# Attention with keys, queries and results stored half by half, and the last inverse moved beside the value products of the first half

## The chip, the cores and the metric

The kernel runs on one core of one Trainium2 chip. The metric is the device time in microseconds (us) of one execution. Before the change, three runs took 573.23, 575.68 and 578.89 us, a median of 575.68 us. A difference of about 1% is what a measurement of this kernel can tell from no change.

## The reference

Two independent problems share one launch, and their outputs are concatenated: A in columns 0 to 639, B in columns 640 to 1279.

```python
def _A_ref(x, wqkv, wo):                 # x 1x2048x640, wqkv 640x1920, wo 640x640
    H = 32; Dh = D // H                  # 32 heads of 20
    W, dil = 8, 2                        # 8 keys: positions s, s-2, ..., s-14
    q, k, v = split of (x @ wqkv)
    idx = pos[:, None] - off[None, :]
    mask = idx >= 0
    logits = einsum("bhsd,bhswd->bhsw", q, kg) * scale
    logits = where(mask, logits, -1e9)
    attn = softmax(logits, axis=-1)
    o = einsum("bhsw,bhswd->bhsd", attn, vg)
    return o @ wo

def _B_ref(u, A_re, A_im, B_re, B_im, C_re, C_im, log_dt, Dskip):
    P = exp(dt * A * l)                  # a 2048-tap filter per channel, from 192 modes
    K = einsum("dn,dnl,dn->dl", C, P, dt * B).real
    y = irfft(rfft(u padded) * rfft(K padded))[:L]
    return y + u * Dskip
```

## The kernel before

**The two problems in time.** Problem B comes first: for five chunks of channels the filter is made from tables (about the first 360 us of the profiled execution), its transform and that of `u` are multiplied, and the first part of the inverse (`ia`, line 419) leaves a tensor `Z` that is written to memory as `Zdram`. The second part of the inverse (`ib`, line 566) reads it back in blocks called `zq` and adds the result into `u`. Problem A (class `Attention`, line 599) begins beside the last chunk of B: `x` is loaded and transposed into `xa` (tag `X0`) and `xb` (tag `S8`), and the keys and queries of the first half are projected beside the last `ia`.

**Halves.** The 2048 positions are four segments of 512 that sit side by side in partition groups of 32 heads. Each segment is cut into half 0 (its first 256 positions) and half 1. A key window reaches back 14 positions (`HALO`). `proj_k` (656) and `proj_q` (677) project one half in ten steps each, every step being five matmuls of 128x512 and one copy out of PSUM. For half 0, `proj_k` has five more short steps for the last 14 keys of every segment. `kT` and `qT` hold both halves of a segment in one run of 512 positions.

**`Attention.run` (787) sets the order.** (1) `logits(0, w)` (698) for the eight window positions w: VectorE multiplies queries by shifted keys into `prod` (128x5120, two places, tags `X1` and `M`), and TensorE sums over head elements into `ps_l`. These are interleaved with `other`, which is the 22 steps of `ib`, and then with the ten key steps of half 1. (2) The ten query steps of half 1. (3) `softmax(0)` (713) and `logits(1, w)`, interleaved with the 20 value projections `proj_v(d)` (688). All values go into one tile `v2` (tag `u`), and one DMA then fills its halo. (4) `av(0, b, w)` (751), with `softmax(1)` between the first steps: VectorE multiplies values by weights into `prod2` (three places, tags `Ssp`, `WK`, `A1`), and TensorE sums over w into `ps_o`. There are three blocks b of 8, 8 and 4 head elements, with eight w each. (5) `av(1)`, interleaved with the eight `out_proj` steps (774) of half 0. (6) The `out_proj` steps of half 1, which end the kernel.

**What sets the order on the engines.** `interleave` (342) mixes two lists of steps evenly. The tile framework then fixes one order of instructions for each engine, which can differ a little from the written one, and puts waits where a tile is read, written or its place reused. PSUM is one pool of eight banks in this part (tag `bank`): the logits of a half hold four, the value sums of a block hold four, and `ps_ib`, `ps_qk`, `ps_v` and `ps_op` take what is left.

**`ib` before.** Each step (three positions of 64, 22 steps) is 3 matmuls with the identity, 24 short ones with `H`, and a copy to `u`, by ScalarE and VectorE in turn (`Evac(nc, "ad")`, 562). Every fourth step loads a `zq` block by five DMAs of 192 KB on SyncE's queue. Six blocks share two places (tags `Ssp`, `WK`), so block n + 2 waits until block n is used up. After steps l = 30 and l = 63, four DMAs write `u` to the output.

```python
interleave([self.logits(0, w) for w in range(W)], other + rest)   # 794
for st in self.proj_q(1, new, ev): st()                           # 795
...
interleave(l1, [self.proj_v(d) for d in range(DH)])               # 809
...
for i, st in enumerate(av(0)):                                    # 816
    st()
    if i % 2 == 1 and i < 8: sm[1 + i // 2]()
interleave(av(1), op(0))                                          # 821
```

Of the kernel before, what the change touches and what calls it, by code (L numbers as in the profile page):

```python
# [18 lines left out]
NCH = 5  # L19
# [414 lines left out]
def partB(tc, pools, prm, B_u, B_Dskip, out_b, att):  # L434
# [164 lines left out]
class Attention:  # L599
# [42 lines left out]
    def load_w(self):  # L642
        nc, ar = self.nc, self.ar
        self.w = {}
        for i, nm, tag in ((1, "k", "WU"), (0, "q", "MX"), (2, "v", "R")):
            t = self.w[nm] = ar.tile([128, 5, D], bf16, name="w" + nm, tag=tag)
            nc.sync.dma_start(out=t[:], in_=self.wsrc[:, :, D * i:D * i + D])
        self.kT = ar.tile([128, 5, HALO + S], bf16, name="kT", tag="Y1")
        nc.gpsimd.memset(self.kT[:, :, 0:HALO], 0.0)
        self.qT = ar.tile([128, 5, S], bf16, name="qT", tag="Y0")  # L650

    def proj(self, w, ct, rhs, ps):
        for kt in range(5):
# [2 lines left out]
    def proj_k(self, hf, new, ev):  # L656

        x4 = lambda kt: self.xs(kt).rearrange("p (s i) -> p s i", s=4)

        def part(ct, sp):  # L660
            def run():
                ps = new()[:].rearrange("p (s i) -> p s i", s=2)
                self.proj("k", ct, lambda kt: x4(kt)[:, 2 * sp:2 * sp + 2, 256 * hf:256 * hf + 256], ps)
                n = 256 - HALO * hf
                k4 = self.kT[:, ct, HALO:HALO + S].rearrange("p (s i) -> p s i", s=4)
                ev(k4[:, 2 * sp:2 * sp + 2, 256 * hf:256 * hf + n], ps[:, :, 0:n])
            return run

        def halo(ct):
            def run():  # L670
                ps = new()[:, 0:4 * HALO].rearrange("p (s i) -> p s i", s=4)
                self.proj("k", ct, lambda kt: x4(kt)[:, :, 512 - HALO:512], ps)
                ev(self.kT[:, ct, HALO:HALO + S].rearrange("p (s i) -> p s i", s=4)[:, :, 512 - HALO:512], ps)
            return run
        return [part(ct, sp) for ct in range(5) for sp in range(2)] + ([halo(ct) for ct in range(5)] if hf == 0 else [])

    def proj_q(self, hf, new, ev):
        x4 = lambda kt: self.xs(kt).rearrange("p (s i) -> p s i", s=4)

        def part(ct, sp):  # L680
            def run():
                ps = new()[:].rearrange("p (s i) -> p s i", s=2)
                self.proj("q", ct, lambda kt: x4(kt)[:, 2 * sp:2 * sp + 2, 256 * hf:256 * hf + 256], ps)
                ev(self.qT[:, ct].rearrange("p (s i) -> p s i", s=4)[:, 2 * sp:2 * sp + 2, 256 * hf:256 * hf + 256], ps)
            return run
        return [part(ct, sp) for ct in range(5) for sp in range(2)]

    def proj_v(self, d):
        def run():
            ps = self.bank("ps_v")  # L690
            for kt in range(5):
                for sc in range(4):
                    self.nc.tensor.matmul(ps[32 * sc:32 * sc + 32, :], lhsT=self.w["v"][:, kt, d:D:DH], rhs=self.xs(kt)[:, 512 * sc:512 * sc + 512],  # L693
                                          start=(kt == 0), stop=(kt == 4), tile_position=(0, 32 * sc), skip_group_check=True)
            self.nc.scalar.copy(out=self.v2[:, d, HALO:HALO + 512], in_=ps[:])
        return run

    def logits(self, hf, w):
        def run():
            if w == 0:  # L700
                self.lps[hf] = [self.bank("ps_l", [128, 2, 256]) for _ in range(4)]
            q4 = self.qT[:].rearrange("p c (s i) -> p c s i", s=4)
            k4 = self.kT[:, :, HALO - DIL * w:HALO - DIL * w + S].rearrange("p c (s i) -> p c s i", s=4)
            pr = self.ar.tile([128, 5, 4, 256], bf16, name="prod", tag=("X1", "M")[w % 2])
            hs = slice(256 * hf, 256 * hf + 256)
            self.nc.vector.tensor_tensor(out=pr[:], in0=q4[:, :, :, hs], in1=k4[:, :, :, hs], op=A.mult)  # L706
# [44 lines left out]
    def av(self, hf, b, w):  # L751
# [5 lines left out]
        def run():  # L757
            if w == 0:
                self.ops[(hf, b)] = [self.bank("ps_o", [128, nd // 4, 256]) for _ in range(4)]
            ops = self.ops[(hf, b)]  # L760
            p2 = self.ar.tile([128, 8, 256], bf16, name="prod2", tag=("Ssp", "WK", "A1")[w % 3])
            off = HALO + 256 * hf - DIL * w
            nc.vector.tensor_tensor(out=p2[:, 0:nd], in0=self.v2[:, 8 * b:8 * b + nd, off:off + 256], in1=self.attn[:, hf, w, :].unsqueeze(1).to_broadcast([128, nd, 256]), op=A.mult)  # L763
            for dq in range(4):
                for sc in range(4):
                    sl = slice(32 * sc, 32 * sc + 32)
# [1 line left out]
                                     tile_position=(32 * sc, 32 * dq), skip_group_check=True)  # L768
            if w == W - 1:
                for sc in range(4):  # L770
                    nc.scalar.copy(out=self.o4[:, sc, 2 * b:2 * b + nd // 4, 256 * hf:256 * hf + 256], in_=ops[sc][:])
        return run

    def out_proj(self, hf, sc, q):
        def run():
            s0 = 256 * hf + 128 * q
            ob = self.ar.tile([128, D], bf16, name="ob", tag="PF", bufs=2)
            for eh in range(2):
                ps = self.bank("ps_op", [128, 320])
                for dd in range(5):  # L780
                    self.nc.tensor.matmul(ps[:], lhsT=self.o4[:, sc, dd, s0:s0 + 128], rhs=self.wo[:, dd, 320 * eh:320 * eh + 320], start=(dd == 0), stop=(dd == 4))  # L781
                self.nc.scalar.copy(out=ob[:, 320 * eh:320 * eh + 320], in_=ps[:])
            r0 = 512 * sc + s0
            self.nc.sync.dma_start(out=self.out_a[r0:r0 + 128, :], in_=ob[:])
        return run

    def run(self, psa, other):
# [5 lines left out]
        rest = self.proj_k(1, new, ev)  # L793
# [16 lines left out]
        nc.gpsimd.memset(self.v2[0:32, :, 0:HALO], 0.0)  # L810
        nc.sync.dma_start(out=self.v2[32:128, :, 0:HALO], in_=self.v2[0:96, :, 512:512 + HALO])
# [75 lines left out]
```

## Time and profile before

| | before |
|---|---|
| three runs, us | 573.23, 575.68, 578.89 |
| profiled execution, us | 571.97 |
| its span in the profile, us | 570.2 |
| TensorE matmul busy | 430.1 us, 75% |
| TensorE weight load busy | 266.7 us, 47% |
| VectorE busy | 410.3 us, 72% |
| ScalarE busy | 342.3 us, 60% |
| mean granted TensorE clock | 0.924 |

The profiled execution took 1.8 us more than its span, and it lies 3.7 us under the median of the three runs. Times in views are in us from the start of the span, and a line such as L706 is a line of the kernel before. Of a busy figure, a matmul's end is modelled, so a busy TensorE need not be at its peak. "Idle before" is the time an engine stood still ahead of an instruction, with the instruction that released it.

### The profile page before, as it was taken

To read this page: it belongs to the slowest core of one execution; us is meant where nothing else is said; L and a number is where in the kernel's file an instruction comes from. 1 tells how busy PE (TensorE), PEld (TensorE's weight loads), DVE (VectorE), ACT (ScalarE), POOL (GpSimd) and SP (SyncE) were. 2 spreads that over 40 slices of the span, in tenths; PEclk is the share of its full clock that TensorE was granted. 3 is DMA by queue.
4 is the path that set the end of the run, shared out by engine and by line. 5 is a ranking of instruction groups with operands and counts; after the bars stand their busy time and mean duration, and the time that the engine had idled before them with its cause. 6 is when DMAs were issued, how large, how long until landed. Compare 5 with 4: busy or idle time off the path is not lost.

```text
span 570.2 us, 15418 instructions
## 1 busy us (share of the span) xinstructions
PE 430.1 (75%) x6929; PEld 266.7 (47%) x6929; DVE 410.3 (72%) x501; ACT 342.3 (60%) x449; POOL 35.2 (6%) x49
## 2 busy tenths in 40 slices
PE   0135794798889798888988887899785679835796
PEld 0013463364556465546554555656552347701354
DVE  3574799869886998699976977232962669699880
ACT  2483683979597969595977595375221534421354
POOL 8700000000000000100000000000000000000000
PEclk9999997899899999899997999799798899955799
DMA  4594324350035203612052059205472150000112
GB/s 118 128 162 168 119 76 151 91 137 12 11 82 159 85 6 81 171 56 82 2 175 49 3 183 264 77 6 190 154 177 92 29 108 15 5 2 1 36 56 98
DMA packets 51674, 51.56 MB, mean 90 GB/s; under 512 B 37384, under 2 KB 48328, under 8 KB 48664
## 3 DMA queue, kind: packets, MB, share of 16 engines
q1 hardware_dynamic: 49720, 49.69, 31.9%
q0 software_dynamic: 1184, 0.89, 0.7%
q8 instruction: 54, 0.88, 0.6%
q10 hardware_dynamic: 704, 0.00, 0.1%
q14 instruction: 12, 0.10, 0.1%
HBM read 32.30 MB, written 18.19 MB: 89 GB/s over the span
## 4 chain that ended last, share of the span: by engine, by line
PE 29%; DVE 9%; ACT 7%; issue 6%; DMA 2%; SPq 0%; ACTq 0%; POOL 0%; DVEq 0%
PE ps_qk L654 7%; PE ps_v L693 4%; DVE prod L763 3%; PE ps_k L289 3%; PE ps_op L781 2%; DVE prod L706 2%; PE ps_k L286 2%; PE ps_ib L583 2%; ACT Y L248 2%; PE ps_l L709 2%; ACT X L248 1%; PE ps_ia L426 1%; PE ps_t L202 1%; PE ps_xt L634 1%; PE ps_ib L577 1%
## 5 line engine op out<-in xcount | busy, mean ns | idle before, releaser
L706 DVE TENSOR_TENSOR prod<-qT,kT 128x5120 bf16<-128x5120 bf16 x16 | 44.7, 2822 | 25.1 <-ACT kT L337 14.3
L248 ACT ACTIVATE X<-ps_t 128x1024 bf16<-128x1024 int16 x60 | 60.6, 1045 | 3.0 <-PE ps_t L202 2.3
L248 ACT ACTIVATE Y<-ps_t 128x1024 bf16<-128x1024 int16 x60 | 59.2, 1041 | 1.2 <-PE ps_t L202 0.6
L202 PE MATMUL ps_t<-R,PF 128*128 128x512 f16 (+1 forms) x160 | 51.8, 421 | 8.4 <-ACT X L248 3.7
L286 PE MATMUL ps_k<-Y,X 128*32 128x64 bf16 x1280 | 51.8, 294 | 2.1 <-issue 1.8
L289 PE MATMUL ps_k<-Y,X 64*32 64x64 bf16 x1280 | 47.7, 291 | 4.4 <-issue 2.4
L763 DVE TENSOR_TENSOR prod<-v,attn 128x2048 bf16<-128x2048 bf16 (+1 forms) x48 | 46.8, 1039 | 3.2 <-PE ps_o L767 2.7
L202 PE MATMUL ps_t<-R,PM 128*128 128x256 f16 (+4 forms) x120 | 23.4, 299 | 33.0 <-DMA PM<-scr 22.5
L337 DVE CAST A<-ps_f 128x1024 bf16<-128x1024 f32 x28 | 34.2, 1220 | 15.4 <-PE ps_f L376 15.2
L337 ACT CAST Ssp<-ps_f 128x1024 bf16<-128x1024 f32 x26 | 26.5, 1021 | 30.5 <-PE ps_f L387 23.1
L289 PEld LDWEIGHTS <-X 64*32 64x32 bf16 x1280 | 34.5, 109 | 19.3 <-issue 16.8
L286 PEld LDWEIGHTS <-X 128*32 128x32 bf16 x1280 | 34.2, 109 | 18.1 <-issue 11.6
L254 DVE TENSOR_TENSOR Y<-Y,M 128x2048 bf16<-128x2048 bf16 x30 | 36.6, 1219 | 6.1 <-ACT Y L248 6.0
L767 PE MATMUL ps_o<-prod,ident 32*32 32x512 bf16 (+1 forms) x768 | 22.5, 453 | 23.8 <-DVE prod L763 23.7
L376 PE MATMUL ps_f<-BD,u 128*64 128x128 bf16 x320 | 23.1, 296 | 22.9 <-DVE A L337 10.3
L256 DVE TENSOR_TENSOR Y<-Y,M 128x2048 bf16<-128x2048 bf16 x30 | 36.6, 1221 | 0.4
L260 DVE TENSOR_TENSOR X<-X,MX 128x2048 bf16<-128x2048 bf16 x30 | 36.6, 1219 | 0.2
L222 ACT ACTIVATE M<-ps_t 128x1024 bf16<-128x1024 f32 x30 | 30.0, 1026 | 8.8 <-DVE Y L256 4.3
L376 PEld LDWEIGHTS <-u 128*64 128x64 bf16 x320 | 20.8, 204 | 27.3 <-issue 27.1
L205 PE MATMUL ps_t<-R,PF 128*64 128x512 f16 (+1 forms) x160 | 25.4, 384 | 5.5 <-ACT Y L248 3.4
L202 PEld LDWEIGHTS <-PM 128*128 128x128 f16 (+1 forms) x120 | 8.6, 102 | 42.8 <-DMA PM<-scr 22.5
L337 DVE CAST Ssp<-ps_f 128x1024 bf16<-128x1024 f32 x14 | 17.1, 1220 | 12.6 <-PE ps_f L387 12.6
(150 smaller groups left out, 852.6 us busy)
## 6 DMA issues: line engine op xcount, KB each, us to landing
Udram<-Ssp SPq DMA_DIRECT2D x5, 1024.0 KB
U<-Udram SPq DMA_DIRECT2D x5, 1024.0 KB
Uw<-Udram SPq DMA_DIRECT2D x10, 512.0 KB
Zdram<-Z SPq DMA_DIRECT2D x5, 1024.0 KB
zq<-Zdram SPq DMA_DIRECT2D x25, 192.0 KB
u<-in_B_u_dram SPq DMA_DIRECT2D x4, 640.0 KB
xn<-in_A_x_dram SPq DMA_DIRECT2D x4, 640.0 KB
out_dram<-ob SPq DMA_DIRECT2D x16, 160.0 KB
```

Source lines behind the costliest of these rows:

```text
L202: MM(ps, lhsT=Pt[0:K, 2 * blk + th, 0:128], rhs=rhs[0:K], start=True, stop=True, skip_group_check=True)
L248: order(nc.scalar.activation(out=dst, in_=ps[:].bitcast(i16)[:, :, 0::2], func=ACT.Sin, scale=SINSC))
L254: V.tensor_tensor(out=hi, in0=lo, in1=m(0), op=A.mult)
L256: V.tensor_tensor(out=lo, in0=lo, in1=m(2), op=A.mult)
L260: V.tensor_tensor(out=xf, in0=xf, in1=mx, op=A.mult)
L286: MM(o, lhsT=X[:, r, g, t], rhs=Y[:, r, g, :, t], start=(k == 0 and r == 0), stop=False, tile_position=(0, 32 * g), skip_group_check=True)
L289: MM(o, lhsT=X[hb:hb + 64, r, 4 + g % 2, t], rhs=Y[hb:hb + 64, r, 4 + g % 2, :, t], start=False, stop=(r == 1), tile_position=(hb, 32 * g) ...
L337: ins = self.nc.scalar.copy(out=out, in_=in_) if e == "a" else self.nc.vector.tensor_copy(out=out, in_=in_)
L376: MM(ps[64 * r:64 * r + 64, i], lhsT=src_fn(8 * q + i), rhs=BD[:, r], start=(i % 4 == 0), stop=True, skip_group_check=True, tile_position= ...
L654: self.nc.tensor.matmul(ps, lhsT=self.w[w][:, kt, 128 * ct:128 * ct + 128], rhs=rhs(kt), start=(kt == 0), stop=(kt == 4))
L706: self.nc.vector.tensor_tensor(out=pr[:], in0=q4[:, :, :, hs], in1=k4[:, :, :, hs], op=A.mult)
L763: nc.vector.tensor_tensor(out=p2[:, 0:nd], in0=self.v2[:, 8 * b:8 * b + nd, off:off + 256], in1=self.attn[:, hf, w, :].unsqueeze(1).to_bro ...
```

## The change

- `kT`, `qT` and `o4` get an outer index for the half, so each half is a separate run of memory. The keys of half 1 get their own 14 halo columns, which one new ScalarE copy (`mid`, 128x280) fills from half 0; the short key steps cover three segments instead of four.
- `ib` leaves the first stage: `logits(0)` is now interleaved with the ten key and the ten query steps of half 1, and `ib` is interleaved with `av(0)` and `softmax(1)`.
- `zq` now uses the places of `xa` and `xb` (`X0`, `S8`). Every copy of `ib` to `u` is now ScalarE's.
- `v2` becomes three tiles (8, 8 and 4 head elements, tags `Ssp`, `WK`, `MX`), each with its own halo DMA as soon as it is full. `prod2` uses `X1`, `M` and `Y1`.

```diff
-    evy = Evac(nc, "ad")
+    evy = Evac(nc, "a")
-                zt[0] = z = ar.tile([...], name="zq", tag=("Ssp", "WK")[l // NP % 2])
+                zt[0] = z = ar.tile([...], name="zq", tag=("X0", "S8")[l // NP % 2])
-        self.kT = ar.tile([128, 5, HALO + S], bf16, name="kT", tag="Y1")
+        self.kT = ar.tile([128, 2, 5, 4, HALO + 256], bf16, name="kT", tag="Y1")
-        self.qT = ar.tile([128, 5, S], bf16, name="qT", tag="Y0")
+        self.qT = ar.tile([128, 2, 5, 4, 256], bf16, name="qT", tag="Y0")
+        def mid():
+            self.nc.scalar.copy(out=self.kT[:, 1, :, :, 0:HALO], in_=self.kT[:, 0, :, :, 256:256 + HALO])
-            self.nc.scalar.copy(out=self.v2[:, d, HALO:HALO + 512], in_=ps[:])
+            if d % 8 == 0:
+                self.v2.append(self.ar.tile([128, min(8, DH - d), HALO + 512], bf16, name="v2", tag=("Ssp", "WK", "MX")[d // 8]))
+            v2 = self.v2[d // 8]
+            self.nc.scalar.copy(out=v2[:, d % 8, HALO:HALO + 512], in_=ps[:])
+            if d in (7, 15, 19):
+                self.nc.gpsimd.memset(v2[0:32, :, 0:HALO], 0.0)
+                self.nc.sync.dma_start(out=v2[32:128, :, 0:HALO], in_=v2[0:96, :, 512:512 + HALO])
-            p2 = self.ar.tile([128, 8, 256], bf16, name="prod2", tag=("Ssp", "WK", "A1")[w % 3])
+            p2 = self.ar.tile([128, 8, 256], bf16, name="prod2", tag=("X1", "M", "Y1")[w % 3])
-        interleave([self.logits(0, w) for w in range(W)], other + rest)
-        for st in self.proj_q(1, new, ev):
-            st()
+        interleave([self.logits(0, w) for w in range(W)], self.proj_k(1, new, ev) + self.proj_q(1, new, ev))
+        a0 = []
         for i, st in enumerate(av(0)):
-            st()
+            a0.append(st)
             if i % 2 == 1 and i < 8:
-                sm[1 + i // 2]()
+                a0.append(sm[1 + i // 2])
+        interleave(a0, other)
-        self.o4 = ar.tile([128, 4, 5, 512], bf16, name="o4", tag="Y0")
+        self.o4 = ar.tile([128, 2, 4, 5, 256], bf16, name="o4", tag="Y0")
```

More of the change, by code (lines that the diff above doesn't have):

```diff
@@ L569, in run @@
                 np_ = min(NP, 64 - l)
-                zt[0] = z = ar.tile([128, NCH, 2 * NP, 32], bf16, name="zq", tag=("Ssp", "WK")[l // NP % 2])
+                zt[0] = z = ar.tile([128, NCH, 2 * NP, 32], bf16, name="zq", tag=("X0", "S8")[l // NP % 2])
                 for c in range(NCH):
@@ L647, in load_w @@
             nc.sync.dma_start(out=t[:], in_=self.wsrc[:, :, D * i:D * i + D])
-        self.kT = ar.tile([128, 5, HALO + S], bf16, name="kT", tag="Y1")
-        nc.gpsimd.memset(self.kT[:, :, 0:HALO], 0.0)
-        self.qT = ar.tile([128, 5, S], bf16, name="qT", tag="Y0")
+        self.kT = ar.tile([128, 2, 5, 4, HALO + 256], bf16, name="kT", tag="Y1")
+        nc.gpsimd.memset(self.kT[:, 0, :, 0, 0:HALO], 0.0)
+        self.qT = ar.tile([128, 2, 5, 4, 256], bf16, name="qT", tag="Y0")
     def proj(self, w, ct, rhs, ps):
@@ L663, in run @@
                 self.proj("k", ct, lambda kt: x4(kt)[:, 2 * sp:2 * sp + 2, 256 * hf:256 * hf + 256], ps)
-                n = 256 - HALO * hf
-                k4 = self.kT[:, ct, HALO:HALO + S].rearrange("p (s i) -> p s i", s=4)
-                ev(k4[:, 2 * sp:2 * sp + 2, 256 * hf:256 * hf + n], ps[:, :, 0:n])
+                ev(self.kT[:, hf, ct, 2 * sp:2 * sp + 2, HALO:HALO + 256], ps)
             return run
@@ L670, in run @@
             def run():
-                ps = new()[:, 0:4 * HALO].rearrange("p (s i) -> p s i", s=4)
-                self.proj("k", ct, lambda kt: x4(kt)[:, :, 512 - HALO:512], ps)
-                ev(self.kT[:, ct, HALO:HALO + S].rearrange("p (s i) -> p s i", s=4)[:, :, 512 - HALO:512], ps)
-            return run
-        return [part(ct, sp) for ct in range(5) for sp in range(2)] + ([halo(ct) for ct in range(5)] if hf == 0 else [])
+                ps = new()[:, 0:3 * HALO].rearrange("p (s i) -> p s i", s=3)
+                self.proj("k", ct, lambda kt: x4(kt)[:, 0:3, 512 - HALO:512], ps)
+                ev(self.kT[:, 0, ct, 1:4, 0:HALO], ps)
+            return run
+        def mid():
+            self.nc.scalar.copy(out=self.kT[:, 1, :, :, 0:HALO], in_=self.kT[:, 0, :, :, 256:256 + HALO])
+        return [part(ct, sp) for ct in range(5) for sp in range(2)] + ([halo(ct) for ct in range(5)] if hf == 0 else [mid])
     def proj_q(self, hf, new, ev):
@@ L683, in run @@
                 self.proj("q", ct, lambda kt: x4(kt)[:, 2 * sp:2 * sp + 2, 256 * hf:256 * hf + 256], ps)
-                ev(self.qT[:, ct].rearrange("p (s i) -> p s i", s=4)[:, 2 * sp:2 * sp + 2, 256 * hf:256 * hf + 256], ps)
+                ev(self.qT[:, hf, ct, 2 * sp:2 * sp + 2], ps)
             return run
@@ L701, in run @@
                 self.lps[hf] = [self.bank("ps_l", [128, 2, 256]) for _ in range(4)]
-            q4 = self.qT[:].rearrange("p c (s i) -> p c s i", s=4)
-            k4 = self.kT[:, :, HALO - DIL * w:HALO - DIL * w + S].rearrange("p c (s i) -> p c s i", s=4)
             pr = self.ar.tile([128, 5, 4, 256], bf16, name="prod", tag=("X1", "M")[w % 2])
-            hs = slice(256 * hf, 256 * hf + 256)
-            self.nc.vector.tensor_tensor(out=pr[:], in0=q4[:, :, :, hs], in1=k4[:, :, :, hs], op=A.mult)
+            self.nc.vector.tensor_tensor(out=pr[:], in0=self.qT[:, hf], in1=self.kT[:, hf, :, :, HALO - DIL * w:HALO - DIL * w + 256], op=A.mult)
             for ct in range(5):
@@ L760, in run @@
             ops = self.ops[(hf, b)]
-            p2 = self.ar.tile([128, 8, 256], bf16, name="prod2", tag=("Ssp", "WK", "A1")[w % 3])
+            p2 = self.ar.tile([128, 8, 256], bf16, name="prod2", tag=("X1", "M", "Y1")[w % 3])
             off = HALO + 256 * hf - DIL * w
-            nc.vector.tensor_tensor(out=p2[:, 0:nd], in0=self.v2[:, 8 * b:8 * b + nd, off:off + 256], in1=self.attn[:, hf, w, :].unsqueeze(1).to_broadcast([128, nd, 256]), op=A.mult)
+            nc.vector.tensor_tensor(out=p2[:, 0:nd], in0=self.v2[b][:, :, off:off + 256], in1=self.attn[:, hf, w, :].unsqueeze(1).to_broadcast([128, nd, 256]), op=A.mult)
             for dq in range(4):
@@ L770, in run @@
                 for sc in range(4):
-                    nc.scalar.copy(out=self.o4[:, sc, 2 * b:2 * b + nd // 4, 256 * hf:256 * hf + 256], in_=ops[sc][:])
+                    nc.scalar.copy(out=self.o4[:, hf, sc, 2 * b:2 * b + nd // 4], in_=ops[sc][:])
         return run
@@ L775, in run @@
         def run():
-            s0 = 256 * hf + 128 * q
+            s0 = 128 * q
             ob = self.ar.tile([128, D], bf16, name="ob", tag="PF", bufs=2)
@@ L780, in run @@
                 for dd in range(5):
-                    self.nc.tensor.matmul(ps[:], lhsT=self.o4[:, sc, dd, s0:s0 + 128], rhs=self.wo[:, dd, 320 * eh:320 * eh + 320], start=(dd == 0), stop=(dd == 4))
+                    self.nc.tensor.matmul(ps[:], lhsT=self.o4[:, hf, sc, dd, s0:s0 + 128], rhs=self.wo[:, dd, 320 * eh:320 * eh + 320], start=(dd == 0), stop=(dd == 4))
                 self.nc.scalar.copy(out=ob[:, 320 * eh:320 * eh + 320], in_=ps[:])
-            r0 = 512 * sc + s0
+            r0 = 512 * sc + 256 * hf + s0
             self.nc.sync.dma_start(out=self.out_a[r0:r0 + 128, :], in_=ob[:])
@@ L792, in run @@
         ev = Evac(nc, "a")
-        rest = self.proj_k(1, new, ev)
-        interleave([self.logits(0, w) for w in range(W)], other + rest)
-        for st in self.proj_q(1, new, ev):
-            st()
+        interleave([self.logits(0, w) for w in range(W)], self.proj_k(1, new, ev) + self.proj_q(1, new, ev))
         self.wo = ar.tile([128, 5, D], bf16, name="wo4", tag="WU")
@@ L800, in run @@
             nc.sync.dma_start(out=self.wo[32 * dq:32 * dq + 32], in_=wsrc[dq])
-        self.v2 = ar.tile([128, DH, HALO + 512], bf16, name="v2", tag="u")
+        self.v2 = []
         sm = self.softmax(0)
@@ L809, in run @@
         interleave(l1, [self.proj_v(d) for d in range(DH)])
-        nc.gpsimd.memset(self.v2[0:32, :, 0:HALO], 0.0)
-        nc.sync.dma_start(out=self.v2[32:128, :, 0:HALO], in_=self.v2[0:96, :, 512:512 + HALO])
-        self.o4 = ar.tile([128, 4, 5, 512], bf16, name="o4", tag="Y0")
+        self.o4 = ar.tile([128, 2, 4, 5, 256], bf16, name="o4", tag="Y0")
         av = lambda hf: [self.av(hf, b, w) for b in range(3) for w in range(W)]
```

## The prediction

> **What bounds the kernel now.** I read the groups of instructions by line first, then the chain of work that ended last, then VectorE's timeline from 400 us on, then busy time and granted clock in stretches. Everything before 400 us (tables, transforms, first half's projections) keeps its instructions but for a few short ones, so the sum is about the last 170.2 us (399.96 to 570.2).
>
> From the groups (count, busy us, mean ns, then idle before and its releasers):
>
> ```profile
> L706 DVE TENSOR_TENSOR prod<-qT,kT 128x5120 bf16<-128x5120 bf16 x16 | 44.7, 2822 | 25.1 <-ACT kT L337 14.3
> L763 DVE TENSOR_TENSOR prod<-v,attn 128x2048 bf16<-128x2048 bf16 (+1 forms) x48 | 46.8, 1039 | 3.2 <-PE ps_o L767 2.7
> ```
>
> VectorE lost 25.1 us ahead of the key products, 14.3 us of it to ScalarE's copies into `kT`. The chain shows where:
>
> ```profile
> 425.57 2.17 PE ps_qk L654 x10
> 427.77 0.57 ACT kT L337
> 428.36 2.83 DVE prod L706
> ...
> 433.60 0.57 ACT kT L337
> 434.21 2.13 PE ps_qk L654 x5
> 436.37 0.57 ACT kT L337
> 436.98 1.25 PE ps_qk L654 x5
> 438.26 0.57 ACT kT L337
> 438.87 1.25 PE ps_qk L654 x5
> 440.14 0.57 ACT kT L337
> 440.74 2.84 DVE prod L706
> ```
>
> Two things are seen. Products of half 0 (428.36, 440.74) wait for key copies of half 1, since both lie in one run of `kT`. And TensorE and ScalarE alternate (1.25 + 0.57, a step each 1.88 us instead of 1.08): only one PSUM bank is left, because six banks hold `ib` steps whose `zq` is not there yet (they run at 457.21, 128 matmuls in 2.32 us). VectorE's timeline around it:
>
> ```profile
> 428.36 2.82 DVE L706 TENSOR_TENSOR prod<-qT,kT 128x5120 bf16<-128x5120 bf16 x1 [4.72 <-ACT kT L337]
> 440.74 2.83 DVE L706 TENSOR_TENSOR prod<-qT,kT 128x5120 bf16<-128x5120 bf16 x1 [9.55 <-ACT kT L337]
> ...
> 465.91 8.30 DVE L706 TENSOR_TENSOR prod<-qT,kT 128x5120 bf16<-128x5120 bf16 x3 [4.72 <-ACT qT L337]
> ...
> 515.05 17.48 DVE L763 TENSOR_TENSOR prod<-v,attn 128x2048 bf16<-128x2048 bf16 x19
> ```
>
> So the stretch from 399.96 to 465.91 (66.0 us) is bound by nothing but waits: VectorE is busy 39.8 us in it. From 465.9 to 495.4 TensorE is nearly full (25.9 of 29.4 us); from 495.4 to 554 VectorE is (55.7 of 58.6 us), with TensorE at 34.8 us.
>
> **The change part by part.** The orders of instructions that the two kernels give each engine show that the eight products of half 0 now wait on no ScalarE copy of `kT`.
>
> *Stage A, logits of half 0 with 20 projections.* TensorE again starts at 402.84, after the first product (399.96 + 2.84). It then does 20 steps of 1.08 us (five matmuls; 425.57: ten in 2.17) and eight sums of 0.66 us: 21.6 + 5.3 = 26.9. Its clock is half after the 3.6 us idle, as the row below shows until 408, which adds 2.4. That is 432.1, plus 0.6 for the last query copy. VectorE's eight products (22.6 us) hide beside it. Softmax 0's first three rows (2.34) stand ahead of the first product of half 1, after the last sum, so that starts at 433.2 instead of 465.91: -32.7. Bounds: with a full clock 1.8 less; at 1.88 us a step, as at 438.26 to 440.14, 16 more. I take the nearer end: no `ib` holds a bank here, so four remain.
>
> *Stage B, logits of half 1, softmax 0, value projections.* Softmax 0 was hidden in stage A's idle time; here VectorE has no such cover. It has 8 x 2.83 = 22.6, and of softmax (2 x 2.34 trees, 2.29, 1.75, 2.29 = 11.0) all but the first 2.34: 31.3, say 31.5, to 464.7. TensorE (20 x 1.08 + 8 x 0.55 = 26.0, plus about 5 of waiting for products and half clock) ends at 466.4. Before it was 29.5 (465.91 to 495.44): +2.0. The values no longer wait for the output DMAs of `u` before their copies (the first sum is done near 470.6, its copy starts at 479.25), but TensorE worked on; worth nothing. Bounds of the stage: +1.8 (31.3 alone) to +4.5 (TensorE's half clock lasting as long again as the 2.4 of stage A). The halo DMA (3.13 us at 496.50) lay beside VectorE's tree and subtraction (495.44 to 500.18) and is worth nothing either; its three successors come earlier, the last one behind two `zq` issues on SyncE's queue, some 20 us before it is needed.
>
> *Stage C, value products of half 0, softmax 1, `ib`.* `ib` costs TensorE 22 x 0.84 us (0.31 + 0.53) = 18.5 us, and ScalarE 22 x 0.56 = 12.3. VectorE loses its 11 copies (6.6 us), which had stood in stage A. VectorE has, to the end of block 1 of half 1, 32 x 1.13 + 8 x 0.6 + 11.0 = 52.0 and remains the bound, if `zq` comes in time. `zq` was loaded ahead at 386.67; now it cannot be issued before the last value projection is done with `xa`. The row to price it: five issues from 409.27, use at 415.82, so 6.5 us from release to use. Block 0 is released at 466.2, there at 472.7 to 473.7. ScalarE meets a new wait: the first `ib` copy stands ahead of softmax 1's exponential, which VectorE's later products wait for. But VectorE has three products, half a tree, two products and the subtraction (10.3) until 475.0, and the first copy is over at 475.2, so this costs 0.2. Behind that, blocks 2 and 3 land at 483.7 and 490, ahead of their use. Block 4 is late: SyncE first issues the four output DMAs of `u` (4.54 us at 418.73), so it is issued at 494.4 and lands at 500.9, block 5 at 501.5. TensorE's order has 128 `ib` matmuls (2.32 us, more at half clock) between the halves of the first products of half 1, so VectorE, three places ahead, stands from 502.8 to 506.4: 3.6 us. Sum: 52.0 + 3.6 + 1.9 of older gaps (the 1.91 at 534.44 falls in the same place, others remain) = 57.5 against 54.5 (495.44 to 549.95): +3.0. Bounds: -3.6 when `zq` is in time; above, see the rivals.
>
> *Stage D, block 2 of half 1.* Before, 6.05 us pass from 549.95 to the last copy of `ps_o` (556.0), with two or three output steps beside it. In the new order ScalarE copies blocks 0 and 1 back to back, and six of the eight output steps of half 0 come after block 1. The tail does eight such steps in 11.6 us: 2.05 + 6 x 1.33 + 1.2 = 11.2, +5.0 (between 0 and +6). The tail from there (14.2 us) is the same.
>
> *Small.* `mid` (128x280 on ScalarE, nearest row the 128x256 copies at 0.3) may push the last transform by 0.4. Fewer halo columns and contiguous rows: nothing, since a product of 5120 takes 2.82 us from strided rows already.
>
> Sum: -32.7 + 2.0 + 3.0 + 5.0 + 0.4 = -22.3. On the profiled execution (571.97) that is 549.7; its median of runs lies 3.7 higher, so I say 553.
>
> **A rule against the row.** After idling, and at light load, TensorE runs at half clock here (columns: stretch, length, busy and count of TensorE, weight loads, VectorE, ScalarE, GpSimd, clock, DMA, GB/s):
>
> ```profile
> 404.00:406.00 2.00, 2.00 (x43) 1.72 (x43) 2.00 (x2) 0.00 (x0) 0.00 (x0) 0.50 0.20 75
> 416.00:418.00 2.00, 2.00 (x78) 1.36 (x68) 1.43 (x2) 0.56 (x1) 0.00 (x0) 1.00 0.82 290
> 516.00:520.00 4.00, 2.25 (x64) 0.60 (x64) 4.00 (x5) 0.00 (x0) 0.00 (x0) 0.50 0.00 0
> ```
>
> The Trainium skill, TensorE: Matmul & The Clock Gate, section "Part 1: The HAM clock gate (the "warmup" mystery)", says that the throttled state is the default and that only a window of about 3.4 us of sustained activity lifts it. Read strictly it speaks against stage C, whose bursts never fill a window: `ib` would stay at half clock. By the rule the sum would be -22.3 + 4.1 = -18 (4.1 is worked out under rival 1 from rows), by the row at 416 the -22 above. The rest does not need this paragraph.
>
> **The rivals.**
> 1. *Half clock throughout stage C.* For it: 0.50 at 516 to 520 with 2.25 of 4 us busy. Against: 1.00 at 416 with `ib` in the stream. Price: an `ib` step at half clock is 1.35 (48 matmuls in 1.78 at 405.08, identities 0.45), so 22 x 1.35 + 16 x 0.66 + 8 x 0.44 = 43.8 from 466.4, and VectorE resumes at 510.5 instead of 506.4: about 557.
> 2. *`zq` bound.* Each place is refilled twice behind its use; at 10 us instead of 6.5, three loads on one place cost 10.5: about 563. Against: nothing else loads then.
> 3. *Banks again.* Projections at 1.88 us in stage A: 553 + 16 = 569. Against: nothing holds banks.
> 4. *Better.* No `zq` stall and no bunched output steps: -3.6 and -5.0, about 544.5.
> 5. *Slower than before.* The `zq` refill again, one mechanism: the place `X0` is loaded three times in series, so the gain of 22.3 is gone at 6.5 + 22.3 / 3 = 13.9 us a load, and beyond that it is slower; at 16 us it is 582. Against: twice the only turn-around that the trace shows.
>
> That the change does not do what it says is rival 3: the wait on `kT` is gone by the order, the pace need not be.
>
> **How the numbers follow.** Likeliest 0.57 (own range 547 to 559), rival 1 0.12, rival 2 0.10, rival 3 0.05, rival 4 0.13, rival 5 0.03. The range leaves out rivals 3 and 5 and the far ends of 2 and 4: 544 to 564. All but rival 5 and a part of 3 are faster by over 1% (about what a measurement of this kernel can tell from no change): faster 0.95, same 0.02, slower 0.03.
>
> **What would show it.** Right: no idle before L706 by `kT`; the first product of half 1 near 433, the first value product near 465, block 1 of half 1 done near 522; one stop of 3 to 4 us in VectorE near 503, released by `ib`. Wrong: steps of 1.9 us in stage A (rival 3); clock 0.5 from 475 to 500 (rival 1); TensorE waiting for `zq` several times (rivals 2, 5); VectorE stopping at the tree of softmax 1, if the first `zq` lands after 475.

## The result, and the profile after

The kernel after took 551.39 us (median of four runs, 547.59 to 553.15) beside 574.45 us of the kernel before (four runs): a ratio of 0.9619, 95% interval 0.9526 to 0.9712. Two more series gave 0.9666 (0.9594 to 0.9738) and 0.9649 (0.9615 to 0.9683), so by these ratios the gain is 19 to 22 us. One run of the first repeat, 556.13 us, was in a slower state and is left out of its ratio. The forecast was 553 us, 0.961 of the 575.68 us it started from, and faster was right. The profiled execution has a span of 545.8 us. It is the fastest of its series; two repeats have spans of 552.0 and 551.0.

The groups of the kernel after (L710 and L767 are L706 and L763 of before):

```profile
L767 DVE TENSOR_TENSOR prod<-v,attn 128x2048 bf16<-128x2048 bf16 (+1 forms) x48 | 47.5, 1040 | 12.3 <-PE ps_o L771 12.3
L710 DVE TENSOR_TENSOR prod<-qT,kT 128x5120 bf16<-128x5120 bf16 x16 | 44.5, 2817 | 6.7 <-ACT qT L337 4.7
```

Ahead of the key products 25.1 us of idle time became 6.7 (10.3 and 9.1 in the repeats), and `kT` is gone from the releasers. Ahead of the value products 3.2 us became 12.3. The busy times are what they were.

The chain of waits through the first stage (start, us, what):

```profile
396.96 2.84 DVE prod L710
...
399.84 0.73 PE ps_l L713 x20
400.57 3.34 PE ps_qk L654 x15
403.92 0.66 PE ps_l L713 x20
404.58 3.34 PE ps_qk L654 x15
...
414.43 3.34 PE ps_qk L654 x15
417.77 0.69 PE ps_l L713 x20
```

Where before the chain went from TensorE to a ScalarE copy and back at every step, it now stays on TensorE: fifteen projection matmuls in 3.34 us are three steps of 1.11 us, not of 1.88. No `kT` copy stands in it.

VectorE's timeline (start, us, instruction, count, idle time before and its releaser):

```profile
396.96 11.03 DVE L710 TENSOR_TENSOR prod<-qT,kT 128x5120 bf16<-128x5120 bf16 x4 [4.70 <-ACT qT L337]
...
428.57 5.55 DVE L710 TENSOR_TENSOR prod<-qT,kT 128x5120 bf16<-128x5120 bf16 x2
...
458.90 3.49 DVE L767 TENSOR_TENSOR prod<-v,attn 128x2048 bf16<-128x2048 bf16 x3
...
496.23 3.50 DVE L767 TENSOR_TENSOR prod<-v,attn 128x2048 bf16<-128x2048 bf16 x3 [1.66 <-PE ps_o L771]
504.72 1.23 DVE L767 TENSOR_TENSOR prod<-v,attn 128x2048 bf16<-128x2048 bf16 x1 [4.99 <-PE ps_o L771]
...
526.22 1.90 DVE L767 TENSOR_TENSOR prod<-v,attn 128x1024 bf16<-128x1024 bf16 x3 [3.97 <-PE ps_o L771]
```

The first product of half 1 starts at 428.57 (before: 465.91), and half 0's first value product at 458.90. Then two stops appear that the kernel before did not have: 4.99 us ahead of 504.72 and 3.97 us ahead of 526.22. TensorE's timeline shows the first:

```profile
499.78 0.63 PE L771 MATMUL ps_o<-prod,ident 32*32 32x512 bf16 x8 [0.51 <-DVE prod L767]
500.11 0.31 PE L583 MATMUL ps_ib<-zq,H 32*32 32x160 bf16 x2
500.16 0.68 PE L771 MATMUL ps_o<-prod,ident 32*32 32x512 bf16 x8
500.22 4.15 PE L583 MATMUL ps_ib<-zq,H 32*32 32x160 bf16 x118
```

The last `ib` steps run in one piece of 4.15 us among the sums of the first two products of half 1; eight matmuls of these sums come behind it. TensorE waits for no DMA there. In stage C it waits 2.1 us for `zq`, in two places near 467 and 477. TensorE's timeline at the second stop:

```profile
521.65 4.20 PE L785 MATMUL ps_op<-wo,o 128*128 128x320 bf16 x20 [0.71 <-ACT o L775]
525.78 0.72 PE L771 MATMUL ps_o<-prod,ident 32*32 32x256 bf16 x48
```

Twenty matmuls of two output steps stand ahead of the sums of block 2 that VectorE waits for. They take 4.20 us without a wait between them, at a granted clock of 0.50 from 522 to 524, where ten take 1.53 us at clock 1.00 (510.40). In the kernel before only ten stand there, and VectorE stops for 0.52 us. ScalarE waits in these microseconds for a result DMA to free one of the two places of `ob` (1.25 us, until 525.63), and the sums do not wait for that.

The stages, with the prediction's bounds (C of before starts at 495.44, as the prediction has it; C ends with the run of VectorE products that ends block 1 of half 1, D with the last copy of `ps_o`):

| us | before | predicted | after | 1st repeat | 2nd repeat |
|---|---|---|---|---|---|
| start of the first key product | 399.96 | +0.4 | 396.96 | 398.29 | 396.73 |
| A | 65.95 | 33.2 | 31.61 | 34.49 | 33.29 |
| B | 29.53 | 31.5 | 30.33 | 31.21 | 31.22 |
| C | 54.51 | 57.5 | 63.35 | 63.68 | 64.71 |
| D | 6.05 | 11.2 | 9.59 | 9.75 | 10.92 |
| tail | 14.20 | 14.2 | 13.96 | 14.58 | 14.13 |
| A to the end | 170.24 | 147.6 | 148.84 | 153.71 | 154.27 |

A, B, D and the tail came within 1.6 us of the prediction. C grew by 9 to 10 us and not by 3.

### The profile page after: what moved, and what is told of

Read it like the earlier page. It is cut to its first block, busy times and chain, and to the rows that moved or that the text cites. A ratio compares the mean times of both kernels' runs of the same rounds, so it can differ in the third digit from the quotient of the medians.

```text
span 545.8 us, 15408 instructions
## 1 busy us (share of the span) xinstructions
PE 425.0 (78%) x6929; PEld 265.4 (49%) x6929; DVE 404.1 (74%) x490; ACT 347.2 (64%) x461; POOL 35.4 (6%) x51
## 4 chain that ended last, share of the span: by engine, by line
PE 24%; DVE 10%; ACT 8%; issue 7%; DMA 3%; SPq 0%; ACTq 0%; POOL 0%; DVEq 0%; POOLq 0%
PE ps_qk L654 7%; DVE prod L710 3%; PE ps_k L289 3%; DMA out_dram<-ob 2%; PE ps_k L286 2%; DVE prod L767 2%; ACT Y L248 2%; ACT X L248 2%; PE ps_o L771 1%; PE ps_ia L426 1%; PE ps_ib L583 1%; PE ps_t L202 1%; PE ps_xt L634 1%; ACT Ssp L337 1%; PE ps_v L694 1%
## 5 line engine op out<-in xcount | busy, mean ns | idle before, releaser
L767 DVE TENSOR_TENSOR prod<-v,attn 128x2048 bf16<-128x2048 bf16 (+1 forms) x48 | 47.5, 1040 | 12.3 <-PE ps_o L771 12.3
L710 DVE TENSOR_TENSOR prod<-qT,kT 128x5120 bf16<-128x5120 bf16 x16 | 44.5, 2817 | 6.7 <-ACT qT L337 4.7
L289 PEld LDWEIGHTS <-X 64*32 64x32 bf16 x1280 | 34.5, 109 | 18.5 <-issue 16.0
L286 PEld LDWEIGHTS <-X 128*32 128x32 bf16 x1280 | 34.3, 109 | 17.8 <-issue 11.3
L376 PE MATMUL ps_f<-BD,u 128*64 128x128 bf16 x320 | 23.1, 297 | 21.1 <-DVE A L337 10.3
L376 PEld LDWEIGHTS <-u 128*64 128x64 bf16 x320 | 20.9, 205 | 25.3 <-issue 25.1
L202 PEld LDWEIGHTS <-PF 128*128 128x128 f16 (+1 forms) x160 | 13.7, 102 | 26.2 <-issue 21.0
```

Source lines behind the costliest of these rows:

```text
L202: MM(ps, lhsT=Pt[0:K, 2 * blk + th, 0:128], rhs=rhs[0:K], start=True, stop=True, skip_group_check=True)
L286: MM(o, lhsT=X[:, r, g, t], rhs=Y[:, r, g, :, t], start=(k == 0 and r == 0), stop=False, tile_position=(0, 32 * g), skip_group_check=True)
L289: MM(o, lhsT=X[hb:hb + 64, r, 4 + g % 2, t], rhs=Y[hb:hb + 64, r, 4 + g % 2, :, t], start=False, stop=(r == 1), tile_position=(hb, 32 * g) ...
L376: MM(ps[64 * r:64 * r + 64, i], lhsT=src_fn(8 * q + i), rhs=BD[:, r], start=(i % 4 == 0), stop=True, skip_group_check=True, tile_position= ...
L710: self.nc.vector.tensor_tensor(out=pr[:], in0=self.qT[:, hf], in1=self.kT[:, hf, :, :, HALO - DIL * w:HALO - DIL * w + 256], op=A.mult)
L767: nc.vector.tensor_tensor(out=p2[:, 0:nd], in0=self.v2[b][:, :, off:off + 256], in1=self.attn[:, hf, w, :].unsqueeze(1).to_broadcast([128, ...
```

## The experiments

Ratios are to the kernel before in the same series, with 95% intervals; stages are of one profile each.

### The kernel after, twice more

> The changed kernel once more, as the measure for the runs beside it. Its own profile has the first key product at 396.96 us, 3.0 us earlier than before, in a part whose instructions the change leaves alone. If that is scatter from run to run, this run's start moves by 1 to 4 us again while the stages behind it keep their lengths within 1 us (31.6, 30.4, 61.4, 11.5 and 14.0 us). If the change did bring it, the start stays near 397.

> The changed kernel once more, beside the next three. Its two series so far gave ratios to the kernel before of 0.962 and 0.967; 0.96 to 0.97 again is expected by every theory. In the trace the stop of about 5 us near 500 and one of about 4 us near 526 should stand again.

Measured: 552.53 us (0.9666, 0.9594 to 0.9738) and 550.24 us (0.9649, 0.9615 to 0.9683). Both stops are there in both (5.22 and 5.51 us, and 4.09 and 5.38 us near 531). The start of stage A is what differs most between the profiles. TensorE's timeline of the first repeat:

```profile
401.17 1.26 PE L713 MATMUL ps_l<-prod,Gs 128*32 128x256 bf16 x20 [3.53 <-DVE prod L710]
...
408.06 0.73 PE L713 MATMUL ps_l<-prod,Gs 128*32 128x256 bf16 x20
```

After 3.53 us without work the same twenty matmuls take 1.26 us and later 0.73; in the first profile they took 0.73 from the start. The granted clock was 0.50 from 402 to 406 here and 1.00 there. With the second sum late, A is 34.5 instead of 31.6.

### The storage alone

```diff
 # the kernel before, with the changed kT, qT, o4, proj_k, proj_q, logits and out_proj
-        self.kT = ar.tile([128, 5, HALO + S], bf16, name="kT", tag="Y1")
+        self.kT = ar.tile([128, 2, 5, 4, HALO + 256], bf16, name="kT", tag="Y1")
 # ib stays in interleave([logits(0, w)], other + rest)
```

> The kernel before with keys, queries and results stored half by half, and nothing else changed. My theory: the two causes of the first stage are separate, the waits on kT (14.3 us) and the PSUM banks that ib holds while its zq is late. Storage alone takes the first and leaves the second, and the value copies still wait for the output DMAs of u: about 9 us faster than before (6 to 13), with projection steps of 1.9 us still to be seen. Rival, storage is the whole gain: 20 us or more. Rival, storage is nothing without the move: under 3 us.

Measured: 558.91 us, 0.9783 (0.9711 to 0.9856). A is 57.63 us (before 65.95), B from there to the softmax 1 tree 31.8, and C, D and the tail are as before. The products' group (L704 is L706 of before) and a piece of the chain:

```profile
L704 DVE TENSOR_TENSOR prod<-qT,kT 128x5120 bf16<-128x5120 bf16 x16 | 44.5, 2819 | 16.4 <-ACT qT L337 10.8 <-PE ps_l L707 5.5
```

```profile
421.72 0.31 PE ps_ib L577 x3
422.03 0.52 PE ps_ib L583 x24
...
422.87 0.66 PE ps_l L707 x20
...
442.29 11.51 PE ps_qk L654 x45
453.82 0.59 ACT qT L337
454.44 2.88 DVE prod L704 x2
```

The wait on `kT` is gone, but `ib` fills TensorE until 425. The projections start only there, and nine of the ten query steps come in one piece of 11.51 us, behind a key copy that ScalarE made after the exponential of softmax 0. Steps of 1.9 us, expected to stay, are seen only twice (429.21 and 431.12); from 433 to 439 a step takes 1.08 us. The gain by the ratio is 12.4 us (8.2 to 16.5), in the expected range.

### The move alone

```diff
 # the kernel after, with kT, qT, o4 and their users as before
-        self.kT = ar.tile([128, 2, 5, 4, HALO + 256], bf16, name="kT", tag="Y1")
+        self.kT = ar.tile([128, 5, HALO + S], bf16, name="kT", tag="Y1")
```

> The changed kernel with keys, queries and results in one run of memory, as before; ib stays moved. My theory: the waits of products on key copies come back four times, between the third and the tenth key step, each for a product and two or three copies: the first stage is 9 to 10 us longer than in the changed kernel, all else equal, so 12 us faster than before. Rival, with ib gone the copies are always ahead: the same as the changed kernel within 2 us. Rival, all the gain was storage: the time of before.

Measured: 563.97 us, 0.9908 (0.9867 to 0.9949). A is 44.55 us, 10 to 13 more than with both parts; the rest is like the kernel after. VectorE's timeline (L712 is L710):

```profile
396.25 2.83 DVE L712 TENSOR_TENSOR prod<-qT,kT 128x5120 bf16<-128x5120 bf16 x1 [4.77 <-ACT qT L337]
403.84 2.83 DVE L712 TENSOR_TENSOR prod<-qT,kT 128x5120 bf16<-128x5120 bf16 x1 [4.76 <-ACT kT L337]
407.81 2.83 DVE L712 TENSOR_TENSOR prod<-qT,kT 128x5120 bf16<-128x5120 bf16 x1 [1.15 <-ACT kT L337]
417.04 2.82 DVE L712 TENSOR_TENSOR prod<-qT,kT 128x5120 bf16<-128x5120 bf16 x1 [6.40 <-ACT kT L337]
421.01 8.29 DVE L712 TENSOR_TENSOR prod<-qT,kT 128x5120 bf16<-128x5120 bf16 x3 [1.15 <-ACT kT L337]
```

With one run of keys VectorE waits again for copies of half 1, 13.5 us in all. The gain by the ratio is 5.2 us, not the 12 that were expected. In stage A storage takes away 8.3 us, the move 21.4, both 31.5 to 34.3, so neither part alone reaches the length of both. What the move loses is in C (65.3 us, before 54.5) and D (10.8 us, before 6.1). From the first key product on, storage alone gives 6.5 us, the move alone 5.4, both together 16.0 to 21.4. By the ratios of one series it is 12.4, 5.2 and 19.0 us, so that both give more than the sum of the two is not shown.

### The halo of the values at the end

```diff
-            if d in (7, 15, 19):
+            if d == 19:
+                for v2 in self.v2:   # memset and halo DMA of all three tiles
```

> The changed kernel with the three halo DMAs of the values issued together after the last value projection, instead of each as its tile is full. My theory: the second value product needs the halo and now stands until it lands, 3.1 us behind its issue: 4 to 5 us slower than the changed kernel, as a stop of VectorE near 460. In the prediction the halo DMA of the kernel before was worth nothing, since softmax work covered it. Rival: it is still covered, same time.

Measured: 550.70 us, 0.9654 (0.9599 to 0.9709), as the kernel after. But this tells nothing of the cover: SyncE issued the first halo DMA at 445.35 (kernel after: 445.30) and the last at 462.29 (461.50). The framework put them where their tiles were full, whatever the program said, so a late halo was not tried. What the three tiles of `v2` are worth by themselves stays open.

### Copies of `ib` by ScalarE and VectorE in turn

```diff
-    evy = Evac(nc, "a")
+    evy = Evac(nc, "ad")
```

> The changed kernel with the copies of ib to u by ScalarE and VectorE in turn, as before. My theory: VectorE bounds the stage of value products, so its 11 copies of 0.65 us come back nearly whole: 5 us slower than the changed kernel (3 to 7). Rival: VectorE waits 12 us for ps_o there, the copies fit into these waits and free ScalarE earlier: within 1.5 us.

Measured: 551.66 us, 0.9686 (0.963 to 0.9743), not told apart from the kernel after. In the profile C is 67.84 us, 3.1 to 4.5 over the three profiles of the kernel after; VectorE is busy 59.7 of the 67.8 us (kernel after 54.2 of 63.4). So the copies' move to ScalarE is worth 3 to 4.5 us in the stage. In this profiled execution the first key product starts at 392.40, in code that is alike, and that hides it; whether the same holds for the other three runs is not seen.

### Where `u` is written

```diff
 # all of u after the last step
-            if l in (30, 63):
-                a0, a1 = (0, 33) if l == 30 else (33, 64)
+            if l == 63:
+                a0, a1 = (0, 64)
```

> The changed kernel with all output DMAs of u behind the last ib step; the first four no longer stand ahead of zq blocks 4 and 5 on SyncE's queue. In the order of TensorE the last 128 ib matmuls are then spread over the value products instead of standing in one piece. My theory: the stop of VectorE near 500 (5.0 us) goes, 4 us faster than the changed kernel; the output steps of half 0 stay bunched, since eight writes of u now stand ahead of theirs. Rival, zq is late in any case: the stop stays, as TensorE waiting for zq.

Measured: 547.89 us, 0.961 (0.9561 to 0.9659). VectorE's timeline:

```profile
499.93 3.50 DVE L767 TENSOR_TENSOR prod<-v,attn 128x2048 bf16<-128x2048 bf16 x3 [1.22 <-PE ps_o L771]
503.60 10.31 DVE L767 TENSOR_TENSOR prod<-v,attn 128x2048 bf16<-128x2048 bf16 x9 [0.17 <-PE ps_o L771]
...
526.27 1.90 DVE L767 TENSOR_TENSOR prod<-v,attn 128x1024 bf16<-128x1024 bf16 x3 [5.50 <-PE ps_o L771]
```

The stop near 500 is gone: with the writes out of SyncE's way, all `ib` steps run before the sums of half 1, and C is 60.82. TensorE now waits for `zq` there (0.61 and 1.48 us), which is what the rival expected, but VectorE loses 1.22 us and not 5. The second stop stays, 5.50 us, behind the same twenty output matmuls, which take 5.49 us here. SyncE issues the four writes from 500.59 to 511.67 and the first result DMA only at 511.77. D is 11.04.

```diff
 # the writes of u issued by GpSimd
-                    nc.sync.dma_start(out=dst[g, :, a0:a1, :], in_=u[...])
+                    nc.gpsimd.dma_start(out=dst[g, :, a0:a1, :], in_=u[...])
```

> The changed kernel with the output DMAs of u on GpSimd's queue, at the same places. The ib matmuls are spread as in the run with u written last, and the output steps of half 0 come at the places they have in the kernel before. My theory: both new losses go, the stop near 500 (4 us) and the bunched output steps (4 us): 8 us faster than the changed kernel. Rival: TensorE is the bound by now, so what is spread is only paid elsewhere: under 3 us. Rival: DMAs issued by GpSimd cost more than they free: slower.

Measured: 555.43 us, 0.9729 (0.9661 to 0.9797). D is back at 6.06, with ten output matmuls ahead of the sums of block 2, but C is 70.46, and the 8 us that were expected did not come. TensorE's timeline, and VectorE's:

```profile
492.10 0.38 PE L577 MATMUL ps_ib<-u,ident 128*128 128x160 bf16 x3
499.28 0.69 PE L583 MATMUL ps_ib<-zq,H 32*32 32x160 bf16 x13 [6.80 <-DMA zq<-Zdram]
```

```profile
500.61 0.69 DVE L767 TENSOR_TENSOR prod<-v,attn 128x1024 bf16<-128x1024 bf16 x1 [7.61 <-PE ps_o L771]
```

SyncE issues block 4 of `zq` from 486.48, and it is usable at 499.28, 12.8 us later; block 0 of the kernel after took 7.1 (460.45 to 467.58). Now TensorE waits for a DMA, since its order has these matmuls before the copy of block 2. GpSimd's four writes were issued from 485.05 on and landed 6.8 us after issue (median). The Trainium skill, DMA: Bandwidth & Descriptors, section "Queues, rings and completion order", says that a DMA engine takes turns between the queues that have work for it, a packet at a time. This fits loads that are slowed beside writes from another queue, but no run isolates it.

### Four places for the output rows

```diff
-            ob = self.ar.tile([128, D], bf16, name="ob", tag="PF", bufs=2)
+            ob = self.ar.tile([128, D], bf16, name="ob", tag=("PF", "PM")[q], bufs=2)
```

> The changed kernel with four places for output rows instead of two. My theory: of the 5.4 us that the stage of block 2 of half 1 grew, ScalarE's waits for output DMAs (8.8 us in all from 520 us on) are the cause; with four places they go and output steps are less bunched: 3 us faster than the changed kernel, the tail unchanged, since TensorE bounds it with 10 matmuls a step. Rival: the tail is bound by these waits too: 5 us or more.

Measured: 550.50 us, 0.965 (0.9591 to 0.9708), as the kernel after. D is 5.96, as before the change, but the tail is 18.11. ScalarE's timeline:

```profile
528.69 1.20 ACT L775 CAST o<-ps_o 128x256 bf16<-128x256 f32 x4 [3.95 <-PE ps_o L771]
529.75 2.12 ACT L786 CAST ob<-ps_op 128x320 bf16<-128x320 f32 x6
```

With more places the framework moved four output steps of half 0 behind the last copy of `ps_o`: 24 copies of `ob` stand there instead of 16. Ten output matmuls stand ahead of the sums of block 2, and VectorE's second stop is 1.20 us; the end waits for the same steps.

### The writes of `u` put later in the program

```diff
-            if l in (30, 63):
-                ... four writes of that half of u
+            if l == 63:
+                write_u(0, 33)
...
         interleave(av(1), op(0))
+        late()                        # write_u(33, 64)
```

> The first half of u is written after the last inverse step, the second half after the eight output steps of half 0 in the program; nothing else is changed. Theory: both late stops come from the order into which the writes of u on SyncE's queue push other work: 128 inverse matmuls behind the first products of half 1 (5.0 us) and six output steps behind block 1 (4.0 us, waiting for output DMAs). In this kernel's order only 32 inverse matmuls stand behind, and the output steps stand 2, 3 and 3 between the blocks. So the first stop falls to about 1 us, the second to under 1 us, some 7 us faster than the changed kernel: ratio 0.950 or so. Rival: the writes are as long on the queue as before and now alternate with the result DMAs, so that the output steps wait for their places and the tail grows by 3 to 5 us: equal to the changed kernel, 0.960 to 0.967.

Measured: 543.67 us, 0.9546 (0.9512 to 0.958); the kernel after in the same series 0.9649 (0.9615 to 0.9683), 6.6 us more. VectorE's timeline (L769 is L767):

```profile
505.76 10.31 DVE L769 TENSOR_TENSOR prod<-v,attn 128x2048 bf16<-128x2048 bf16 x9 [1.96 <-PE ps_o L773]
516.23 5.30 DVE L769 TENSOR_TENSOR prod<-v,attn 128x2048 bf16<-128x2048 bf16 x6 [0.16 <-PE ps_o L773]
522.05 1.90 DVE L769 TENSOR_TENSOR prod<-v,attn 128x1024 bf16<-128x1024 bf16 x3 [0.53 <-PE ps_o L773]
```

The stops of 4.99 and 3.97 became 1.96 and 0.53. C is 61.87, D 6.06 and the tail 14.11, so the tail did not pay for it, and the rival falls. What the edit did on SyncE's queue is seen in its timeline, of the kernel after and then of this one:

```profile
484.50 4.57 SPq L590 DMA_DIRECT2D out_dram<-u  x4
489.18 9.74 SPq L572 DMA_DIRECT2D zq<-Zdram  x10
```

```profile
485.25 0.34 SPq L569 DMA_DIRECT2D out_dram<-u  x1
486.94 3.63 SPq L577 DMA_DIRECT2D zq<-Zdram  x5
490.62 0.43 SPq L569 DMA_DIRECT2D out_dram<-u  x1
491.97 4.04 SPq L577 DMA_DIRECT2D zq<-Zdram  x5
496.05 1.04 SPq L569 DMA_DIRECT2D out_dram<-u  x2
```

The writes of the first half are late in the program only. The framework issued one ahead of the loads of block 4, one ahead of those of block 5 and two behind, instead of all four ahead of both. So the gain belongs to this order of the queue and the order on TensorE that came with it, not to writing late. Ten output matmuls, not twenty, stand ahead of the sums of block 2.

> The same with four places for output rows instead of two. Theory of a queue that holds the output steps: with four places ScalarE need not wait for a result DMA that stands behind a write of u, and another 1 to 2 us go (ratio 0.947). Rival: the tail is bound by TensorE's ten matmuls a step and gives it back, as four places alone (ratio 0.965) showed: equal to the run with two places within 1 us.

The edit is the one above together with the four places. Measured: 541.79 us, 0.9506 (0.9471 to 0.9541), the best kernel of the study; the interval overlaps that of two places, so these 1.9 us are not settled. C is 58.41, D 6.05, the tail 13.16: in this order the extra places no longer lengthen the tail.

### Does half clock cost anything in stage C?

```diff
 # on the kernel with u written late
-            for i in range(n):
+            for i in [*range(n)] * 3:
                 MM(ps[:, 160 * i:160 * i + 160], lhsT=pools["ident"][:], rhs=u[:, l + i, :], start=(i == 0), ...)
```

> As the run with the late writes, and the three identity matmuls of each inverse step are issued three times over (the sum starts anew each time, so the values stay), 128 more matmuls of 128x160 at 0.10 to 0.13 us, 13 to 16 us of TensorE work between 458 and 504. Question: does the half clock of TensorE in stage C cost anything? Theory A (it does, 3 to 4 us): more work keeps the clock nearer 1 and the small waits on ps_o go, so that the time is equal to or up to 2 us better than with the late writes alone. Theory B (VectorE is the bound there and the half clock is hidden): the clock rises, VectorE's gaps do not shrink, and where TensorE is close to full the added work shows, 0 to 6 us slower than with the late writes alone.

Measured: 545.65 us, 0.9565 (0.9535 to 0.9595), beside 0.9546 without. One stretch over most of stage C, of the kernel without and then of the one with the extra matmuls (stretch, length, busy us and count of TensorE, weight loads, VectorE, ScalarE, GpSimd, clock, DMA share, GB/s):

```profile
459.00:518.00 59.00, 44.35 (x1278) 27.03 (x1270) 51.51 (x49) 25.73 (x51) 0.00 (x0) 0.88 0.49 132
```

```profile
459.00:518.00 59.00, 49.19 (x1416) 33.71 (x1409) 51.66 (x48) 27.25 (x53) 0.00 (x0) 0.97 0.47 129
```

The clock rose from 0.88 to 0.97, and C is the same (61.67 beside 61.87). This speaks for theory B: VectorE is the bound, and with this order the half clock lies beside it. It does not rule out that a gain from the clock and the cost of the added matmuls cancel, for VectorE waits 6.4 us for `ps_o` in C without them and 7.2 with them.

## Why the prediction was right, and where it was not

*Stage A, -32.7.* Measured -34.3, -31.5 and -32.7. The working holds: projections beside the products, no bank shortage (steps of 1.11 us), and the half clock after the idle, priced at 2.4 us, which makes 1.7 to 2.9 us between the three profiles. The first profile had none of it (clock 1.00 from 400 to 428), so that its A is 1.6 us under the forecast is luck. The prediction called the old stretch bound by nothing but waits; TensorE was busy 50.2 of its 66.0 us, and the kernel with the move alone shows what it is worth to take `ib` out of it. That neither part alone gives this stage is shown by the two kernels with one of them (57.63 and 44.55 us).

*Stage B, +2.0.* Measured +0.8, +1.7, +1.7. Softmax 0 is no longer covered, as said.

*Stage C, +3.0.* Measured +8.8, +9.2, +10.2: this is the term that was mis-sized, at 57.5 instead of 63.4 in the first profile. Three parts make the 5.9. VectorE's own work was 54.2 us and not 52.0: the sum goes to the end of block 1, but the bound that it is compared with, 549.95, lies behind three products of block 2, 1.8 us by its own 0.6 each. The stop was 4.99 and not 3.6, since the piece of `ib` matmuls took 4.15 us; the prediction had 2.32 with "more at half clock" left out of the sum. The other waits are 4.1 us together (1.66, 0.90, 0.53, 0.45, 0.28, 0.16 and smaller) and not 1.9; the 1.66 follows a stop of TensorE itself, 2.13 us at 493.76, that nothing in the profile explains. The granted clock shows the half clock:

```profile
480.00:484.00 4.00, 2.22 (x71) 1.52 (x75) 3.99 (x4) 0.08 (x1) 0.00 (x0) 0.50 0.29 93
...
500.00:504.00 4.00, 4.00 (x127) 3.67 (x113) 0.00 (x0) 1.67 (x3) 0.00 (x0) 0.51 0.03 8
504.00:508.00 4.00, 4.00 (x88) 2.47 (x80) 2.75 (x3) 2.41 (x6) 0.00 (x0) 1.00 0.38 76
...
512.00:516.00 4.00, 2.20 (x56) 1.11 (x41) 4.00 (x5) 2.05 (x4) 0.00 (x0) 1.00 0.61 151
```

Two columns tell the tale at 500: TensorE busy 4.00 of 4 us at clock 0.51, VectorE busy 0. At 480 the clock is the same and VectorE is busy 3.99: there it costs nothing. So rival 1 was true in part and counts only where VectorE waits, which is in the two stops. The rule of the Trainium skill that the prediction weighed (TensorE: Matmul & The Clock Gate, section "Part 1: The HAM clock gate (the "warmup" mystery)") fits the rise to 1.00 after the full stretch. But at 512 the clock is 1.00 with 2.20 of 4 us busy, at 480 it is 0.50 with 2.22 (there TensorE had stood 3.27 us up to 481.78), so load in a stretch alone does not tell the clock. Neither sum, -18 or -22, is decided by three series of -19 to -22 us.

*Why the stop is there.* The prediction said block 4 of `zq` is late behind four writes of `u`, issued at 494.4, and that TensorE's order has 128 `ib` matmuls among the first products of half 1. The order is as it said. The wait is not seen: SyncE issues block 4 from 489.18 on, and TensorE runs these matmuls without waiting for a DMA. With the writes out of the way, the order has them earlier and the stop is gone (4.99 to 1.22 with all writes last), so the writes are its cause, through the order and not through a wait at run time. How late block 4 itself landed in the kernel after is not seen.

*Stage D, +5.0.* Measured +3.5, +3.7, +4.9, by bunched output steps as said. What they cost VectorE is TensorE's time, which the sum, built of ScalarE's copies, did not name: two output steps instead of one ahead of the sums of block 2, in part at half clock, 4.20, 4.32 and 5.39 us in the three profiles. Three edits each give an order with one step there: the writes spread on the queue (D 6.06), the writes by GpSimd (6.06) and four places of `ob` (5.96, paid for by a tail of 18.11). So both the writes and the two places bear on the order; why the framework bunches the steps is not seen. Rival 4, which had neither stop, comes near to a real kernel. Its 544.5 us is 0.946 of 575.68, and the kernels with the writes spread reached 0.9546 and 0.9506. Their 543.67 and 541.79 us lie below 544.5 since the kernel before took 569.69 in that series.

*Start and `mid`, +0.4.* The first key product came 1.7 to 3.2 us earlier. Over the fourteen profiles of this study it comes between 392.40 and 400.41, with nearly the same code ahead of it, so this is scatter, and +0.4 can't be seen in it. In the first profile it hid part of the miss in C: against the prediction -3.4 here, -1.6 in A, -1.2 in B and -1.6 in D stand beside +5.9. From A to the end the repeats took 153.71 and 154.27 us, 6.1 and 6.7 over the predicted 147.6, so the closer agreement of the first profile (148.84) is luck.

Rivals 2, 3 and 5 did not come. TensorE waited 2.1 us for `zq`, the projections kept their pace, and a refill took 7.1 us where 6.5 was assumed.

## What to carry to other kernels

When work is moved beside another stage, price the order that it forces on the queues, and not only its length: here the place of eight output DMAs in one queue, and the order of instructions that came with it, took back 6.6 us of a gain of 26. A single tile that holds two halves ties them together for whoever writes one and reads the other; splitting it and moving the competitor took 8.3 and 21.4 us out of the first stage, but the move gave most of its part back in later ones. An edit that puts a DMA later in the program need not put it later on its queue: read the queue's own timeline before naming a cause. Before adding places, look where the order puts what they free: four places moved about 4 us from one stage into the tail, and no longer did so once the writes were spread.

## What the runs showed of the hardware

- TensorE stood 2.13 us at 493.76 in the kernel after (2.02 and 1.14 in the repeats) without a wait that the profile shows, in the middle of a row of `ps_o` matmuls; clock 0.63 (496 to 500) and 0.51 (500 to 504) follow in the kernel after. The cause is open.
- TensorE's clock fell to 0.50 at 522 to 524 in the kernel after, although from 508 on it had stood no longer than 1.14 us at a time; it was busy 0.88 of the 2 us from 518 to 520, at clock 1.00.
- Twenty 128x256 matmuls after 3.5 us of idle took 0.73 us in one execution (clock 1.00) and 1.26 in another of the same program (clock 0.50); with the projections behind them, stage A differs by up to 2.9 us.
- Four writes of half of `u`, back to back on SyncE's queue, took 4.57 us to issue, and four writes of all of it 11.08 us, 2.8 us each; the queue's next DMA was issued 0.1 us after them. Issued singly between other DMAs, writes of half of `u` took 0.34 and 0.43 us.
- The first key product comes between 392.40 and 400.41 us over all kernels, and the spans of three profiles of one kernel differ by up to 6.2 us. Stage lengths from a common start told the experiments apart where the whole times did not.
